# Attention with hashed masks and two gated layers: a head pair's queries prepared as a whole before its keys

## The chip, the cores and the metric

The kernel runs on one core of a Trainium2 chip. Its time is the device time of one execution in microseconds (us); a run is compared with runs of the other kernel on the same chip. The core has five engines with queues of their own, each in order: TensorE (PE, with its weight loads shown as PEld), VectorE (DVE), ScalarE (ACT), GpSimd (POOL) and SyncE (SP). SP issues all transfers (DMAs) of this kernel.

## The reference

```
q, k, v: 2 x 8 x 768 x 64; proj: 64 x 6
q_bits, k_bits = (q @ proj > 0), (k @ proj > 0)          # six hash bits a token
mask   = bucket(q_bits) == bucket(k_bits)                # all six bits agree
scores = q @ k.T / sqrt(64), -1e9 where not mask
attn   = exp(scores - max); attn /= (sum + 1e-9)
x      = attn @ v, heads side by side                    # 1536 x 512
h = x @ w_in (512 x 2048);   x = (h * cos(h)) @ w_out
g = x @ w_gate (512 x 1536); out = (silu(g) * (x @ w_val)) @ w_out2
```

## The kernel before

The 16 heads are worked in 8 pairs (NPAIR). A pair has 6 units, blocks of 128 queries; unit u belongs to pair u // 6, and each unit does both heads of its pair (j = 0, 1). `att_step(u)` issues one step of a software pipeline: scores of unit u, exponentials of u and u - 1, normalization of u - 1 (`row_norm`, on POOL), transposes of the probabilities of u - 2 (`p_transpose`, four groups of three on TensorE, one of the four copied out of PSUM by VectorE at L481, three by ScalarE), and the products with v for older units. The transposes share two PSUM buffers (`ps_t`), the scores two others (`ps_s`).

A float32 product is made exact enough by splitting an operand into a high part (rounded to float32r) and a low part (the remainder). The score product is two matrix products for each j: X with Y (L429; X holds the high and the low part of the queries, Y the high part of the keys twice) and Z with W (L431; Z holds the queries' high part and the query bits, W the keys' low part and the key bits). The bits are scaled so that a pair of tokens with different hash bits gets a huge negative score.

`prep(pr)` makes X, Y, Z and W of the next pair while the current one is worked. For queries and keys in turn it transposes the loaded rows on TensorE (L243), copies them to `raw` (tiles qT and kT) by ScalarE (L249) or VectorE (L253), and rounds them to `hi` (qH and kH, VectorE, L257). Then eight transfers spread the high parts (L260 to L263), in the order X, Z, Y, Y for one half of the tokens and again for the other. Then TensorE projects both (L285), VectorE compares with zero into the tile `bt` (L289), POOL scales it (L293), and eight small transfers put the bits into Z and W (L308). Last, POOL makes the low parts in place, qT - qH and kT - kH (L314), each with two transfers, to X and to W (L320).

The order on every engine is that of the program text: `prep` is a generator, and `fill` (called four times in a unit) takes one step of it and one step of the building of a dense weight. Before pair pr + 2 is prepared its queries and keys are loaded (`load_pair`, L222, emitted at the fifth unit of a pair). Every third unit from unit 8 on a weight is built, ten in all: ScalarE starts it (L125), VectorE finishes it in three operations (L140, L144, L148), and it is fetched three units earlier (L106, L110). SP therefore issues, in one line, the spreading of a pair, the loads of the one after it, and the weights.

Small per-row vectors (mn, the row maxima; sv, the sums; rv, the reciprocals) live in the pool `sm`.

Of the kernel before, what the change touches and what calls it, by code (L numbers as in the profile page):

```python
# [10 lines left out]
F32 = mybir.dt.float32  # L11
# [3 lines left out]
ALU = mybir.AluOpType  # L15
PSUM = bass.MemoryType.PSUM

P = 128
# [8 lines left out]
def lsh_attention_moe_moe2(  # L27
# [13 lines left out]
    nc = tc.nc  # L41
# [158 lines left out]
    ld = actx.enter_context(tc.tile_pool(name="ld", bufs=1))  # L200
    pre = actx.enter_context(tc.tile_pool(name="pre", bufs=1))
    pp = actx.enter_context(tc.tile_pool(name="pp", bufs=6))
    sm = actx.enter_context(tc.tile_pool(name="sm", bufs=8))

    pj0 = {nm: pre.tile([P, D], F32, tag="pj0" + nm, name="pj0" + nm) for nm in "qk"}
    pjs = pre.tile([P, NB], F32, tag="pjs", name="pjs")
# [20 lines left out]
    def prep_psum(pr, i, name):  # L227
        pool, tag = (ps_v, "av") if pr == 1 and i % 2 else (ps_p, "pp")
        return pool.tile([P, 512], F32, tag=tag, name=name)

    def prep(pr):
# [4 lines left out]
        X, Y, Z, W = (  # L236
            qk.tile([P, 2, S], F32R, tag=nm, bufs=2, name=f"{nm}{pr}") for nm in "XYZW"
        )
        for nm in ("q", "k"):
            for j in range(2):  # L240
                ps = prep_psum(pr, j, f"tr{nm}{pr}_{j}")
                for c in range(HB):
                    nc.tensor.transpose(  # L243
                        ps[:, c * P : (c + 1) * P],
                        nat[nm, pr][:, j, 2 * c : 2 * c + 2, :].rearrange("p c d -> p (c d)"),
                        ident,
                    )
                if nm == "q" or pr == 1:
                    nc.scalar.activation(  # L249
                        out=raw[nm][:, j, :], in_=ps[:, :HALF], func=AF.Copy, scale=TAKEN[nm]  # L250
                    )
                else:
                    nc.vector.tensor_copy(raw[nm][:, j, :], ps[:, :HALF])  # L253
                yield
                if pr > 1:
                    yield
            nc.vector.tensor_copy(hi[nm], raw[nm])  # L257
        for e in range(2):
            r, cs = slice(e * D, (e + 1) * D), slice(e * HALF, (e + 1) * HALF)
            nc.sync.dma_start(out=X[:D, :, cs].bitcast(F32), in_=hi["q"][r].bitcast(F32))  # L260
            nc.sync.dma_start(out=Z[:D, :, cs].bitcast(F32), in_=hi["q"][r].bitcast(F32))
            nc.sync.dma_start(out=Y[:D, :, cs].bitcast(F32), in_=hi["k"][r].bitcast(F32))
            nc.sync.dma_start(out=Y[D:, :, cs].bitcast(F32), in_=hi["k"][r].bitcast(F32))  # L263


        if pr == 1:
            bt = early.tile([P, 2, DM], F32, tag="raw", bufs=2, name="bt1")[:, :, :HALF]
            for j in range(2):
                ps = prep_psum(pr, j, f"pj1_{j}")
                for g, nm in enumerate(("q", "k")):  # L270
                    nc.tensor.matmul(
                        out=ps[g * D : (g + 1) * D, :HALF], lhsT=pj0[nm], rhs=raw[nm][:, j, :],
                        start=True, stop=True,
                    )
                nc.vector.tensor_scalar(
                    out=bt[:, j], in0=ps[:, :HALF], scalar1=0.0, scalar2=cvec[:, 1:2],
                    op0=ALU.is_gt, op1=ALU.subtract,
                )
# [17 lines left out]
        for g, dst in enumerate((Z, W)):  # L296
            rows = slice(D, D + 2 * NB)
            for e in range(2):
                cs = slice(e * HALF, (e + 1) * HALF)
                if pr == 1:  # L300
                    r0 = D * g + 32 * e
                    nc.sync.dma_start(
                        out=dst[rows, :, cs].bitcast(F32), in_=bt[r0 : r0 + 2 * NB]
                    )
                    continue
                for j in range(2):
                    r0 = 32 * (2 * g + j) + 2 * NB * e
                    nc.sync.dma_start(  # L308
                        out=dst[rows, j, cs].bitcast(F32), in_=bt[r0 : r0 + 2 * NB]
                    )  # L310
        yield
        yield
        for nm in ("q", "k"):
            nc.gpsimd.tensor_tensor(  # L314
                out=raw[nm], in0=raw[nm], in1=hi[nm].bitcast(F32), op=ALU.subtract
            )
            for e in range(2):
                cs = slice(e * HALF, (e + 1) * HALF)
# [4 lines left out]
        heads[pr] = (X, Y, Z, W)  # L323

    def prep_first():

# [20 lines left out]
                    )  # L347
            return ps

        def lows(eng, dst, j, nm, hi, e):  # L350
            r, cs = halves[e]
            eng.tensor_tensor(  # L352
                out=dst[:, j, cs], in0=raw[nm][r, j, :], in1=hi[:, j, cs].bitcast(F32),
                op=ALU.subtract,
            )

        ps = transposes(0)
        for j in range(2):
# [27 lines left out]
            lows(nc.gpsimd, W[:D], j, "k", Y[:D], 0)  # L386
            lows(nc.vector, X[D:], j, "q", X[:D], 0)
# [4 lines left out]
            for e in range(2):  # L392
# [8 lines left out]
            lows(nc.vector, W[:D], j, "k", Y[:D], 1)  # L401
            nc.vector.tensor_copy(Z[D : D + 2 * NB, j, :HALF], bt[: 2 * NB, j])
            yield
        for j in range(2):
            r, cs = halves[1]
            for dst in (X, Z):
                nc.scalar.activation(out=dst[:D, j, cs], in_=raw["q"][r, j, :], func=AF.Copy)
            nc.gpsimd.tensor_scalar(
                out=Z[D : D + 2 * NB, j, cs], in0=bt[32 : 32 + 2 * NB, j], scalar1=1.0,
                scalar2=1.0, op0=ALU.mult, op1=ALU.mult,  # L410
            )
            lows(nc.vector, X[D:], j, "q", X[:D], 1)
            yield

    scores = {}
# [469 lines left out]
```

## Time and profile before

| | us |
|---|---|
| median of 3 runs | 821.41 |
| lowest, highest | 819.27, 823.32 |
| the profiled execution | 822.72 |
| its span | 820.9 |
| TensorE busy in the span | 795.2 (97%) |
| VectorE, ScalarE, POOL busy | 466.5, 499.6, 454.1 |

In a row of the profile, L12 is line 12 of the kernel; an operation is named by what it writes and reads (out<-in). In a timeline a row begins with start and duration in us; a figure in square brackets is the idle time of the engine before it and what ended it. "issue" means that the engine waited for nothing that the profile shows by name. Transfers are shown by their issue on SP (SPq), not by their landing.

### The profile page before, as it was taken

How to read it: one execution, taken by the hardware profiler on the slowest of the kernel's cores; microseconds unless marked ns; L12 is line 12 of the kernel's file. 1: busy time of each engine (PE TensorE's matmuls, PEld its weight loads, DVE VectorE, ACT ScalarE, POOL GpSimd, SP SyncE). 2: the span in 40 equal slices, each digit the busy share in tenths (PEclk: the TensorE clock that was granted, in tenths of full speed). 3: DMA queues.
4: the chain of work that ended last, by engine and by line, in shares of the span. 5: the costliest groups of instructions: out<-in, count | busy, mean ns of one | idle time of the engine just before them, and what ended most of it. 6: DMA issues, size and time to landing. Idle time of an engine off the chain costs nothing.

```text
span 820.9 us, 11429 instructions
## 1 busy us (share of the span) xinstructions
PE 795.2 (97%) x3956; PEld 622.6 (76%) x3956; DVE 466.5 (57%) x865; ACT 499.6 (61%) x941; POOL 454.1 (55%) x394
## 2 busy tenths in 40 slices
PE   6899999998999999999999999999999999999998
PEld 4666666666675788888888888888888888888886
DVE  5888987887673999987755688752122111121112
ACT  5777767766685888887767777743334333343332
POOL 4754553653562677677776767744444444445440
PEclk8999999999999999999999999999999999999999
DMA  3745645644502455433220234300001000010001
GB/s 115 179 115 171 168 128 169 172 124 118 149 1 78 129 160 175 154 103 102 79 76 1 63 120 128 101 0 1 1 0 53 1 1 0 1 52 0 1 1 51
DMA packets 47049, 66.52 MB, mean 81 GB/s; under 512 B 3824, under 2 KB 41872, under 8 KB 46992
## 3 DMA queue, kind: packets, MB, share of 16 engines
q1 hardware_dynamic: 46992, 65.80, 27.4%
q8 instruction: 31, 0.51, 0.3%
q14 instruction: 26, 0.21, 0.1%
HBM read 45.09 MB, written 3.15 MB: 59 GB/s over the span
## 4 chain that ended last, share of the span: by engine, by line
PE 86%; DVE 6%; DMA 3%; issue 1%; POOL 1%; ACT 1%; SPq 1%; POOLq 0%; DVEq 0%; ACTq 0%
PE o L608 9%; PE o L610 9%; PE o L609 9%; PE av L491 6%; PE h L608 5%; PE h L610 5%; PE h L609 5%; PE t L473 5%; PE gate L609 4%; PE val L609 4%; PE val L608 4%; PE gate L608 4%; PE gate L610 4%; PE val L610 4%; PE s L429 3%; PE s L431 3%
## 5 line engine op out<-in xcount | busy, mean ns | idle before, releaser
L460 POOL TENSOR_SCALAR p<-p,rv 128x768 f32<-128x768 f32 x96 | 89.4, 942 | 106.3 <-DVE rv L457 99.2
L783 DVE TENSOR_TENSOR u<-val,sg 128x512 f32<-128x512 f32 x36 | 24.9, 692 | 198.7 <-ACT sg L777 188.4
L438 DVE TENSOR_SCALAR_CACHE_REDUCE p<-s 128x768 f32<-128x768 f32 x96 | 91.7, 955 | 46.7 <-PE s L431 38.4
L479 ACT ACTIVATE pt<-t 128x384 f32<-128x384 f32 x144 | 66.9, 486 | 53.6 <-PE t L473 53.5
L449 ACT ACTIVATE p<-p,mn 128x768 f32<-128x768 f32 x96 | 89.6, 934 | 9.4 <-DVE p L438 9.2
L473 PE MATMUL t<-ident,p 128*128 128x128 f32 x576 | 86.2, 274 | 6.0 <-DVE pt L481 5.6
L473 PEld LDWEIGHTS t<-ident,p 128*128 128x128 f32 x576 | 67.4, 140 | 17.1 <-DVE pt L481 7.5
L491 PE MATMUL av<-pt,vn 128*64 128x384 f32 x384 | 72.1, 498 | 0.0
L429 PE MATMUL s<-Y,X 128*128 128x512 f32 x192 | 59.2, 390 | 1.8 <-DVE X L352 1.8
L431 PE MATMUL s<-W,Z 76*128 76x512 f32 x192 | 51.2, 348 | 8.7 <-issue 3.8
L642 ACT ACTIVATE r<-r 128x512 f32<-128x512 f32 x48 | 30.4, 633 | 41.8 <-DVE r L634 41.8
L630 DVE SCALAR_TENSOR_TENSOR rf<-ki,h 128x512 f32<-128x512 int32 x46 | 32.0, 695 | 35.9 <-ACT ki L627 35.6
L429 PEld LDWEIGHTS s<-Y,X 128*128 128x128 f32 x192 | 29.3, 193 | 28.8 <-DVE pt L481 8.4
L125 ACT ACTIVATE w<-raw 128x512 f32<-128x512 f32 x68 | 44.6, 659 | 0.0
L491 PEld LDWEIGHTS av<-pt,vn 128*64 128x64 f32 x384 | 23.4, 136 | 25.8 <-issue 25.8
L654 DVE TENSOR_TENSOR g<-h,r 128x512 f32<-128x512 f32 x48 | 33.1, 689 | 16.9 <-ACT r L643 16.6
L431 PEld LDWEIGHTS s<-W,Z 76*128 76x128 f32 x192 | 30.3, 194 | 15.1 <-issue 7.9
L144 DVE SCALAR_TENSOR_TENSOR bw<-w,bw 128x512 int32<-128x512 int32 x55 | 38.0, 691 | 1.2
L140 DVE TENSOR_SCALAR bw<-raw 128x512 int32<-128x512 int32 x55 | 38.0, 691 | 1.0
L148 DVE SCALAR_TENSOR_TENSOR w<-raw,bw 128x512 int32<-128x512 int32 x55 | 37.5, 683 | 0.9
L643 ACT ACTIVATE r<-r,halfpi 128x512 f32<-128x512 f32 x48 | 34.8, 724 | 1.6
L627 ACT ACTIVATE ki<-h 128x512 int32<-128x512 f32 x48 | 28.3, 590 | 11.2 <-PE h L610 11.2
(1872 smaller groups left out, 2298.7 us busy)
## 6 DMA issues: line engine op xcount, KB each, us to landing
raw<-in_moe_w_out_dram SPq DMA_DIRECT2D x28, 512.0 KB
raw<-in_moe_w_in_dram SPq DMA_DIRECT2D x16, 512.0 KB
raw<-in_moe_w_gate_dram SPq DMA_DIRECT2D x12, 512.0 KB
raw<-in_moe_w_val_dram SPq DMA_DIRECT2D x12, 512.0 KB
Y<-kH SPq DMA_DIRECT2D x28, 192.0 KB
vn<-in_v_dram SPq DMA_DIRECT2D x8, 384.0 KB
out_dram<-ot SPq DMA_DIRECT2D x12, 256.0 KB
qn<-in_q_dram SPq DMA_DIRECT2D x7, 384.0 KB
```

Of the source, the lines that this page charges most:

```text
L125: nc.scalar.activation(out=t, in_=raws[i][:, :, 1].bitcast(F32), func=AF.Copy, scale=2.0**-112)
L429: nc.tensor.matmul(out=ps[:, ks], lhsT=X[:, j, qs], rhs=Y[:, j, ks], start=True, stop=False)
L431: nc.tensor.matmul(out=ps[:, ks], lhsT=Z[:KZ, j, qs], rhs=W[:KZ, j, ks], start=False, stop=True)
L438: nc.vector.tensor_scalar(out=pt, in0=ps[:, :S], scalar1=-MASKED, scalar2=None, op0=ALU.min, op1=ALU.min, accum_out=mn,)
L449: nc.scalar.activation(out=pt, in_=pt, func=AF.Exp, bias=nbias.pop((u, j)), scale=-1.0, accum_out=sums[u][:, j : j + 1],)
L460: nc.gpsimd.tensor_scalar(out=pt, in0=pt, scalar1=rv[:, j : j + 1], scalar2=1.0, op0=ALU.mult, op1=ALU.mult)
L473: nc.tensor.transpose(ps[:, c * P : (c + 1) * P], src[:, kb * P : (kb + 1) * P], ident)
L479: nc.scalar.activation(out=o, in_=s3, func=AF.Copy)
L491: nc.tensor.matmul(out=ps[j * D : (j + 1) * D, :HALF], lhsT=nat["v", pr][:, j, BLOCKS[kb], :], rhs=pts[half, j][:, kb, :], start=(kb == 0) ...
L608: nc.tensor.matmul(out=out_ap, lhsT=sh, rhs=mh, start=first, stop=False)
L609: nc.tensor.matmul(out=out_ap, lhsT=sh, rhs=ml, start=False, stop=False)
L610: nc.tensor.matmul(out=out_ap, lhsT=sl, rhs=mh, start=False, stop=last)
```

## The change

For pairs 2 to 7 `prep` now does all of the queries first: after the rounding of the queries come four transfers (X, X, Z, Z), the low part on POOL and its two transfers, and only then the keys: transposes, copies, rounding, and four transfers to Y. The bits and the keys' low part follow, the latter two steps of the generator earlier against the normalizations. The queries' low part is no longer made in place; it gets a tile of its own (qL, tag `low`, one buffer), and `bt` is now the first half of a tile of the same tag. Pair 1 keeps its order except that of the eight transfers. The pool `sm` has four buffers instead of eight. The two functions `bits` and `lows` hold what stood in the body of `prep`.

```
-    sm = actx.enter_context(tc.tile_pool(name="sm", bufs=8))
+    sm = actx.enter_context(tc.tile_pool(name="sm", bufs=4))
...
             nc.vector.tensor_copy(hi[nm], raw[nm])
-        for e in range(2):
-            r, cs = slice(e * D, (e + 1) * D), slice(e * HALF, (e + 1) * HALF)
-            nc.sync.dma_start(out=X[:D, :, cs].bitcast(F32), in_=hi["q"][r].bitcast(F32))
-            nc.sync.dma_start(out=Z[:D, :, cs].bitcast(F32), in_=hi["q"][r].bitcast(F32))
-            nc.sync.dma_start(out=Y[:D, :, cs].bitcast(F32), in_=hi["k"][r].bitcast(F32))
-            nc.sync.dma_start(out=Y[D:, :, cs].bitcast(F32), in_=hi["k"][r].bitcast(F32))
+            for dst in (X[:D], Z[:D]) if nm == "q" else (Y[:D], Y[D:]):
+                for e in range(2):
+                    r, cs = slice(e * D, (e + 1) * D), slice(e * HALF, (e + 1) * HALF)
+                    nc.sync.dma_start(
+                        out=dst[:, :, cs].bitcast(F32), in_=hi[nm][r].bitcast(F32)
+                    )
+            if pr > 1 and nm == "q":
+                lows(pr, nm, raw, hi)
...
-            bt = pre.tile([P, HALF], F32, tag="bt", name=f"bt{pr}")
+            bt = pre.tile([P, 2, HALF], F32, tag="low", name=f"bt{pr}")[:, 0]
...
+        bits(pr, bt)
         yield
         yield
-        for nm in ("q", "k"):
-            nc.gpsimd.tensor_tensor(
-                out=raw[nm], in0=raw[nm], in1=hi[nm].bitcast(F32), op=ALU.subtract
-            )
-            for e in range(2):
-                cs = slice(e * HALF, (e + 1) * HALF)
-                dst = X[D:, :, cs] if nm == "q" else W[:D, :, cs]
-                nc.sync.dma_start(out=dst.bitcast(F32), in_=raw[nm][e * D : (e + 1) * D])
+        for nm in ("q", "k") if pr == 1 else ("k",):
+            lows(pr, nm, raw, hi)
             yield
             yield
...
+    def lows(pr, nm, raw, hi):
+
+        X, _, _, W = heads[pr]
+        t = raw[nm]
+        if pr > 1 and nm == "q":
+            t = pre.tile([P, 2, HALF], F32, tag="low", name=f"{nm}L{pr}")
+        nc.gpsimd.tensor_tensor(out=t, in0=raw[nm], in1=hi[nm].bitcast(F32), op=ALU.subtract)
+        for e in range(2):
+            cs = slice(e * HALF, (e + 1) * HALF)
+            dst = X[D:, :, cs] if nm == "q" else W[:D, :, cs]
+            nc.sync.dma_start(out=dst.bitcast(F32), in_=t[e * D : (e + 1) * D])
```

On TensorE, VectorE and ScalarE the same instructions stand in the same order; only their waits change. The order differs on POOL and SP, alike for pairs 2 to 7. Shown is the preparation of pair 2.

POOL, from the normalizations of unit 6 on (p are probabilities, rv their reciprocals), before:

```order
L460 TENSOR_SCALAR p_0_536<-p_0_536,rv_605 128x768
L460 TENSOR_SCALAR p_1_578<-p_1_578,rv_605 128x768
L460 TENSOR_SCALAR p_0_602<-p_0_602,rv_669 128x768
L460 TENSOR_SCALAR p_1_639<-p_1_639,rv_669 128x768
L293 TENSOR_SCALAR bt_683<-bt_683,svec 128x384
L314 TENSOR_TENSOR qT_544<-qT_544,qH_545 128x768
L460 TENSOR_SCALAR p_0_666<-p_0_666,rv_752 128x768
L460 TENSOR_SCALAR p_1_725<-p_1_725,rv_752 128x768
L314 TENSOR_TENSOR kT_546<-kT_546,kH_547 128x768
```

and after, the same place:

```order
L473 TENSOR_SCALAR p_0_536<-p_0_536,rv_605 128x768
L473 TENSOR_SCALAR p_1_578<-p_1_578,rv_605 128x768
L332 TENSOR_TENSOR qL_615<-qT_544,qH_545 128x768
L473 TENSOR_SCALAR p_0_602<-p_0_602,rv_677 128x768
L473 TENSOR_SCALAR p_1_647<-p_1_647,rv_677 128x768
L315 TENSOR_SCALAR bt_687<-bt_687,svec 128x384
L332 TENSOR_TENSOR kT_546<-kT_546,kH_547 128x768
L473 TENSOR_SCALAR p_0_674<-p_0_674,rv_756 128x768
L473 TENSOR_SCALAR p_1_729<-p_1_729,rv_756 128x768
```

The queries' subtraction moved up by one unit, and the keys' subtraction moved ahead of the two normalizations that stood before it.

SP, from the weight fetch ahead of the spreading of pair 2 to the loads for pair 3, before:

```order
L110 DMA raw_652<-in_moe_w_in_dram 128x4x256
L260 DMA X_548<-qH_545 64x2x384
L261 DMA Z_550<-qH_545 64x2x384
L262 DMA Y_549<-kH_547 64x2x384
L263 DMA Y_549<-kH_547 64x2x384
L260 DMA X_548<-qH_545 64x2x384
L261 DMA Z_550<-qH_545 64x2x384
L262 DMA Y_549<-kH_547 64x2x384
L263 DMA Y_549<-kH_547 64x2x384
L308 DMA Z_550<-bt_683 12x384 x4
L308 DMA W_551<-bt_683 12x384 x4
L320 DMA X_548<-qT_544 64x2x384 x2
```

and after:

```order
L281 DMA X_548<-qH_545 64x2x384 x2
L281 DMA Z_550<-qH_545 64x2x384 x2
L336 DMA X_548<-qL_615 64x2x384 x2
L110 DMA raw_660<-in_moe_w_in_dram 128x4x256
L281 DMA Y_549<-kH_547 64x2x384 x4
L246 DMA Z_550<-bt_687 12x384 x4
L246 DMA W_551<-bt_687 12x384 x4
L336 DMA W_551<-kT_546 64x2x384 x2
L222 DMA qn_790<-in_q_dram 128x2x384
```

All six transfers of the queries now stand ahead of the keys' and the bits'; the keys' low part (which before followed the last row shown) stands right behind the bits; the second weight fetch went behind the queries.

VectorE at the comparison into bt, with the semaphores that an instruction waits for in square brackets (DMAHW is one of the eight semaphores that the transfers take in turn), before:

```order
L457 RECIPROCAL rv_669<-rv_669 128x2 [waits DVE_49]
L257 CAST kH_547<-kT_546 128x768 [waits DMAHW5_49,DMAHW4_49]
L289 TENSOR_SCALAR bt_683<-pj_684,cvec 128x384 [waits PE_49]
L481 COPY pt_0_660<-t_0_1_701 128x3x128 [waits PE_49]
L140 TENSOR_SCALAR raw_472<-raw_472 128x512 [waits DMAHW4_49,Activation_49]
L438 TENSOR_SCALAR p_1_725,mn_1_726<-s_1_712 128x768 [waits PE_49,Pool_49]
```

and after:

```order
L470 RECIPROCAL rv_677<-rv_677 128x2 [waits DVE_49]
L277 CAST kH_547<-kT_546 128x768 [waits DMAHW7_49,DMAHW6_49]
L311 TENSOR_SCALAR bt_687<-pj_688,cvec 128x384 [waits DMAHW1_49,DMAHW2_49,PE_49,Pool_49]
L494 COPY pt_0_668<-t_0_1_705 128x3x128 [waits PE_49]
L140 TENSOR_SCALAR raw_472<-raw_472 128x512 [waits DMAHW4_49,Activation_49]
L451 TENSOR_SCALAR p_1_729,mn_1_730<-s_1_716 128x768 [waits PE_49]
```

The order is the same, but the comparison has gained the waits for DMAHW1 and DMAHW2, which are here the semaphores of the two transfers X<-qL, and for POOL.

## Rows read from the trace of the kernel before

**Rows 1.** The page, part 4: the chain that ended last, by engine.

```profile
PE 86%; DVE 6%; DMA 3%; issue 1%; POOL 1%; ACT 1%; SPq 1%; POOLq 0%; DVEq 0%; ACTq 0%
```

**Rows 2.** Busy time by stretch: stretch, length, engines (instructions), granted clock, DMA share, GB/s.

```profile
300.00:500.00 200.00, 200.00 (x884) 165.62 (x884) 151.46 (x234) 154.43 (x270) 142.39 (x112) 1.00 0.32 101
```

**Rows 3.** TensorE's groups, 40 to 245 us: busy us, mean ns | idle before, releasers.

```profile
L431 PE MATMUL s<-W,Z 76*128 76x512 f32 (+1 forms) x165 | 43.2, 342 | 6.2 <-issue 3.8 <-DMA qn<-in_q_dram 2.4
...
L243 PE MATMUL trq<-ident,qn 128*128 128x128 f32 x36 | 6.1, 277 | 1.3 <-DMA qn<-in_q_dram 1.3
```

**Rows 4.** Timeline of TensorE at the boundaries before pair 2 and near 190 us.

```profile
67.30 0.62 PE L429 MATMUL s<-Y,X 128*128 128x512 f32 x2
67.75 0.52 PE L431 MATMUL s<-W,Z 76*128 76x512 f32 x2
...
68.68 0.60 PE L429 MATMUL s<-Y,X 128*128 128x512 f32 x2
69.46 0.59 PE L431 MATMUL s<-W,Z 76*128 76x512 f32 x2 [0.18 <-issue]
...
193.16 0.58 PE L431 MATMUL s<-W,Z 76*128 76x512 f32 x2 [2.38 <-DMA qn<-in_q_dram]
```

**Rows 5.** Timeline of SP, the spreading of pair 2: start and time of issue.

```profile
47.65 0.60 SPq L260 DMA_DIRECT2D X<-qH  x1
48.34 1.00 SPq L261 DMA_DIRECT2D Z<-qH  x1
...
57.20 3.24 SPq L308 DMA_DIRECT2D Z<-bt  x4
...
63.58 1.37 SPq L320 DMA_DIRECT2D X<-qT  x2
65.05 1.25 SPq L320 DMA_DIRECT2D W<-kT  x2
```

**Rows 6.** Timeline of POOL in the preparation of pair 2, and pair 7's bit scaling.

```profile
47.20 2.03 POOL L460 TENSOR_SCALAR p<-p,rv 128x768 f32<-128x768 f32 x2 [3.24 <-DVE rv L457]
...
54.15 0.75 POOL L293 TENSOR_SCALAR bt<-bt,svec 128x384 f32<-128x384 f32 x1
54.87 1.83 POOL L314 TENSOR_TENSOR qT<-qT,qH 128x768 f32<-128x768 f32 x1
...
207.26 0.58 POOL L293 TENSOR_SCALAR bt<-bt,svec 128x384 f32<-128x384 f32 x1
```

**Rows 7.** Busy time by stretch, while two and six large transfers run (columns as above).

```profile
49.00:51.00 2.00, 2.00 (x20) 1.73 (x22) 1.73 (x5) 1.50 (x3) 0.24 (x1) 1.00 0.83 184
...
53.50:59.50 6.00, 5.79 (x37) 4.05 (x35) 5.65 (x11) 2.78 (x6) 3.39 (x4) 1.00 0.89 200
```

**Rows 8.** Timeline of VectorE from the comparison of pair 2 on.

```profile
52.43 0.61 DVE L289 TENSOR_SCALAR bt<-pj,cvec 128x384 f32<-128x384 f32 x1
52.96 0.55 DVE L481 COPY pt<-t 128x384 f32<-128x384 f32 x1
53.42 1.03 DVE L140 TENSOR_SCALAR raw<-raw 128x512 int32<-128x512 int32 x1
54.73 0.96 DVE L438 TENSOR_SCALAR_CACHE_REDUCE p<-s 128x768 f32<-128x768 f32 x1 [0.28 <-PE s L431]
...
55.61 1.63 DVE L144 SCALAR_TENSOR_TENSOR w<-w,raw 128x512 int32<-128x512 int32 x1
...
59.05 0.54 DVE L481 COPY pt<-t 128x384 f32<-128x384 f32 x1
```

**Rows 9.** Timeline of TensorE's probability transposes: pair 2, then pair 7.

```profile
54.44 0.82 PE L473 MATMUL t<-ident,p 128*128 128x128 f32 x6
...
59.64 0.55 PE L473 MATMUL t<-ident,p 128*128 128x128 f32 x3 [0.35 <-DVE pt L481]
...
207.54 0.82 PE L473 MATMUL t<-ident,p 128*128 128x128 f32 x6
```

**Rows 10.** Timeline of VectorE at the comparison of pair 7.

```profile
205.54 0.62 DVE L289 TENSOR_SCALAR bt<-pj,cvec 128x384 f32<-128x384 f32 x1
```

More of the change, by code (lines that the diff above doesn't have):

```diff
@@ L229, in prep_psum, with bits @@
         return pool.tile([P, 512], F32, tag=tag, name=name)
+    def bits(pr, bt):
+        _, _, Z, W = heads[pr]
+        rows = slice(D, D + 2 * NB)
+        for g, dst in enumerate((Z, W)):
+            for e in range(2):
+                cs = slice(e * HALF, (e + 1) * HALF)
+                if pr == 1:
+                    r0 = D * g + 32 * e
+                    nc.sync.dma_start(
+                        out=dst[rows, :, cs].bitcast(F32), in_=bt[r0 : r0 + 2 * NB]
+                    )
+                    continue
+                for j in range(2):
+                    r0 = 32 * (2 * g + j) + 2 * NB * e
+                    nc.sync.dma_start(
+                        out=dst[rows, j, cs].bitcast(F32), in_=bt[r0 : r0 + 2 * NB]
+                    )
     def prep(pr):
@@ L235, in prep @@
             hi[nm] = pre.tile([P, 2, HALF], F32R, tag=nm + "H", name=f"{nm}H{pr}")
-        X, Y, Z, W = (
+        X, Y, Z, W = heads[pr] = [
             qk.tile([P, 2, S], F32R, tag=nm, bufs=2, name=f"{nm}{pr}") for nm in "XYZW"
-        )
+        ]
         for nm in ("q", "k"):
@@ L257, in prep @@
             nc.vector.tensor_copy(hi[nm], raw[nm])
-        for e in range(2):
-            r, cs = slice(e * D, (e + 1) * D), slice(e * HALF, (e + 1) * HALF)
-            nc.sync.dma_start(out=X[:D, :, cs].bitcast(F32), in_=hi["q"][r].bitcast(F32))
-            nc.sync.dma_start(out=Z[:D, :, cs].bitcast(F32), in_=hi["q"][r].bitcast(F32))
-            nc.sync.dma_start(out=Y[:D, :, cs].bitcast(F32), in_=hi["k"][r].bitcast(F32))
-            nc.sync.dma_start(out=Y[D:, :, cs].bitcast(F32), in_=hi["k"][r].bitcast(F32))
+            for dst in (X[:D], Z[:D]) if nm == "q" else (Y[:D], Y[D:]):
+                for e in range(2):
+                    r, cs = slice(e * D, (e + 1) * D), slice(e * HALF, (e + 1) * HALF)
+                    nc.sync.dma_start(
+                        out=dst[:, :, cs].bitcast(F32), in_=hi[nm][r].bitcast(F32)
+                    )
+            if pr > 1 and nm == "q":
+                lows(pr, nm, raw, hi)
         if pr == 1:
@@ L295, in prep @@
         )
-        for g, dst in enumerate((Z, W)):
-            rows = slice(D, D + 2 * NB)
-            for e in range(2):
-                cs = slice(e * HALF, (e + 1) * HALF)
[L300 to L310, printed above, removed]
+        bits(pr, bt)
         yield
         yield
-        for nm in ("q", "k"):
-            nc.gpsimd.tensor_tensor(
-                out=raw[nm], in0=raw[nm], in1=hi[nm].bitcast(F32), op=ALU.subtract
-            )
-            for e in range(2):
-                cs = slice(e * HALF, (e + 1) * HALF)
-                dst = X[D:, :, cs] if nm == "q" else W[:D, :, cs]
-                nc.sync.dma_start(out=dst.bitcast(F32), in_=raw[nm][e * D : (e + 1) * D])
+        for nm in ("q", "k") if pr == 1 else ("k",):
+            lows(pr, nm, raw, hi)
             yield
             yield
-        heads[pr] = (X, Y, Z, W)
+    def lows(pr, nm, raw, hi):
[4 more added lines that the diff above has]
+        nc.gpsimd.tensor_tensor(out=t, in0=raw[nm], in1=hi[nm].bitcast(F32), op=ALU.subtract)
+        for e in range(2):
+            cs = slice(e * HALF, (e + 1) * HALF)
+            dst = X[D:, :, cs] if nm == "q" else W[:D, :, cs]
+            nc.sync.dma_start(out=dst.bitcast(F32), in_=t[e * D : (e + 1) * D])
     def prep_first():
@@ L348, in transposes, with rest_of @@
             return ps
-        def lows(eng, dst, j, nm, hi, e):
+        def rest_of(eng, dst, j, nm, hi, e):
             r, cs = halves[e]
@@ L385, in prep_first @@
             yield
-            lows(nc.gpsimd, W[:D], j, "k", Y[:D], 0)
-            lows(nc.vector, X[D:], j, "q", X[:D], 0)
+            rest_of(nc.gpsimd, W[:D], j, "k", Y[:D], 0)
+            rest_of(nc.vector, X[D:], j, "q", X[:D], 0)
             nc.vector.tensor_scalar(
@@ L400, in prep_first @@
                     nc.scalar.activation(out=dst, in_=src, func=AF.Copy, scale=-BIG)
-            lows(nc.vector, W[:D], j, "k", Y[:D], 1)
+            rest_of(nc.vector, W[:D], j, "k", Y[:D], 1)
             nc.vector.tensor_copy(Z[D : D + 2 * NB, j, :HALF], bt[: 2 * NB, j])
@@ L411, in prep_first @@
             )
-            lows(nc.vector, X[D:], j, "q", X[:D], 1)
+            rest_of(nc.vector, X[D:], j, "q", X[:D], 1)
             yield
```

## The prediction

> **What bounds the kernel now.** The chain of work that ended last was read first: 86% of it is TensorE, so a change pays or costs only where TensorE waits [rows 1]. The table by stretch comes second. Between 300 and 500 us TensorE is busy for all 200 us at a granted clock of 1.00, so the two dense layers can neither absorb a delay of the attention nor use up a gain: whatever the attention gains or loses arrives at the end in full [rows 2]. The attention ends near 260 us, and there the waits are small. Third come TensorE's groups between 40 and 245 us. Only two have idle time worth naming: 6.2 us before the second score product (L431, operands W and Z) and 1.3 us before the transposes of the next queries (L243) [rows 3].
>
> The timeline shows what these are. Ordinarily the W-Z product starts 0.45 us after the X-Y product (67.30, 67.75). At the first unit of pair 2 it starts 0.78 us after it (68.68, 69.46) [rows 4]. There the last prepared operands, W from the low part of the keys, were issued only at 65.05 us, behind eight small bit transfers (57.20 on) and the queries' low part (63.58) [rows 5]. The queries of the next pair are loaded behind those again. So the pair boundary is a wait for a late SP queue, six times.
>
> **The change part by part.**
>
> *Relief at the boundary.* The lost time is 0.78 - 0.45 = 0.33 us where the row counts 0.18 us idle: the idle figure misses 0.15 us, because the product before ends late. The 6.2 us are six boundaries and the 1.3 us three, so the loss is 7.5 + 9 x 0.15 = 8.9 us. After the change the queries' low part leaves before the bits, and the keys' low part stands on POOL right behind the bits, ahead of two normalizations. SP then issues in pair 2: bits from about 56.9, eight of them in 6.4 us (57.20 to 63.58), keys' low part at about 63.3 [rows 5]. That is 1.8 us earlier, while TensorE reaches the boundary later (below, 2.3 us). Four microseconds of lead cover every boundary, so I take all 8.9 us. Bounds: 7.5 (the idle figures alone) to 8.9.
>
> *The price: VectorE waits for a transfer.* The queries' low part goes no longer in place but into a tile "low", of which there is one buffer, and the bit tile bt shares it. So the comparison that writes bt (L289, now L311) has to wait until both transfers X<-qL have read that buffer and landed; in the order of the changed kernel it has gained exactly those two waits. VectorE works in order: behind it stand the copy of a transposed block (L481), three weight operations (L140, L144, L148) and the row maxima (L438). TensorE waits for these through its two transpose buffers.
>
> When do they land? The first X<-qH goes out at 47.65 [rows 5]. With all queries together, four transfers follow each other, and the low part joins as fifth and sixth: POOL finishes the normalizations at 47.20 + 2.03 = 49.23 and needs 1.83 us for the subtraction, 51.06 [rows 6]. The six are then limited by the transfer rate: two such transfers (192 KB each) took the 2.0 us from 49.0 to 51.0, and the 6 us with six of them ran at 200 GB/s, a share of 0.89, which is 0.98 us each [rows 7]. Four in a row, issued from 63.58 on, had landed when the product started at 69.46: 5.85 us [rows 4, 5]. Two more make 7.8 us. So the sixth lands at 47.65 + 7.8 = 55.45; with 0.15 us for the waits in a row bt starts at 55.6 instead of 52.43, a delay D of 3.2 us [rows 8].
>
> The Trainium skill ("DMA: Bandwidth & Descriptors", section Bandwidth) states that transfers from SBUF to SBUF are bound by the fabric's 435 GB/s. By it each would take an estimated 0.45 us, the six would be limited by their issue, and the sum would be that of the rival "shorter wait" below; the 200 GB/s of [rows 7] speak against it.
>
> What does D cost TensorE? I replay VectorE from the start B of the comparison [rows 8]. The copy follows at B + 0.53 and is done at B + 1.08. TensorE's fourth transpose group of that unit needs its buffer: it stood at 54.44 + 0.33 = 54.77 [rows 9] and now comes at 55.63 + 1.14 = 56.8, 2.0 us late. Then the weight operations. L140 starts at B + 0.99. Before, it took 1.03 us beside POOL's normalizations and ended 0.3 us after them; now POOL's bit scaling (0.58 us where nothing is beside it [rows 6]) ends at B + 1.23, so L140 ends at B + 1.55. POOL's subtraction for the keys, 1.83 us, then runs to B + 3.4. The row maximum goes from B + 1.55, L144 from B + 2.43. Before, L144 took 1.63 us and ended 0.54 us after POOL's subtraction (54.87 + 1.83); the same lag gives B + 3.95. From its end to the second copy before there are 59.05 - 57.24 = 1.81 us, so this copy starts at B + 5.75. Before it stood at B + 6.62 and already held TensorE up (59.64, idle 0.35) [rows 8, 9]. TensorE thus loses D - 0.87 = 2.3 us a pair. Five pairs (2 to 6) carry weight operations there: 11.5 us. Pair 7 carries none: its comparison at 205.54 moves to 208.74, the copy ends at 209.8, and TensorE's group from 207.54 + 0.33 = 207.87 comes at 209.9, 2.0 us late; nothing further is late [rows 9, 10]. Sum 13.5 us. Bounds: none at all (a wait that is met in time) to five times 3.6 and 2.0, 20 us (the second rival).
>
> *What costs nothing.* Four buffers instead of eight for mn, sv and rv: a vector comes round again after two units (mn) or four (sv, rv), a unit being some 4.9 us (54.77 to 59.64 [rows 9]), and its reader is done within one. POOL's subtraction for the queries, moved up a unit, falls into an idle time of POOL like the 3.24 us before 47.20 [rows 6]. If that cover fell, VectorE could lose up to those 1.83 us, ahead of a comparison that waits anyway. Pair 1 keeps its POOL order; only SP's order within a burst changes, for operands first read at the next boundary. The second weight load of a pair now waits in SP behind the queries; the program fetches it three units ahead of its use, some 15 us.
>
> *Sum.* 13.5 - 8.9 = +4.6 us. On the profiled execution, 822.72 us, that is 827.3; the median of the three runs is 821.41, on which it is 826.0. About 0.5%, 4.1 us, is what a measurement of this kernel can tell from no change, so the forecast is slower, but near that bound.
>
> **The rivals.**
>
> *Shorter wait, no change.* If the low part's transfers overlap the four before instead of queuing behind them, the last one needs only its own time. It is issued at about 51.8, and the lone second transfer needed 51.0 - 48.34 = 2.7 us [rows 5, 7], with completion and waits about 54.9: D is 2.5, a pair loses 1.6 us and the last 1.3, together 9.3, and 821.41 + 0.4 gives 821.8. It decides the sign where D is below about 2.4 us. For it: nothing else is on the queues then. Against it: the full share at 200 GB/s.
>
> *L140 loses to POOL.* If POOL's key subtraction starts before L140, that one waits for the subtraction's end: L140 ends 0.3 us after it at B + 3.7, L144 starts at B + 4.6 and no longer waits (0.6 us), and the second copy stands at B + 7.0. A pair loses 3.6 us, the sum is 20 - 8.9 = +11, 832.5 us. Against it: in [rows 6, 8] L140 ended before the bit scaling went on, which took 0.75 instead of 0.58 us.
>
> *Relief without a price, faster.* If the wait were met in time, 821.41 - 8.9 gives 812.5. It needs the sixth transfer to land by 52.4, 4.8 us after the first is issued; four needed 5.85.
>
> *The change doesn't do what it says.* If the boundary stays late for another reason (a transfer that lags, as at 193.16, with 2.38 us idle the worst of the six [rows 4]), half of the relief is lost: +9, 830.4.
>
> **How the numbers follow.** Forecast as summed (824 to 828.5): 0.48. Shorter wait (820 to 824): 0.22. L140 loses (830 to 834): 0.17. Half the relief: 0.07. No price: 0.06. Slower by over 0.5% means above 825.5: 0.31 of the forecast's 0.48 and the two dear rivals, 0.55. Within 0.5%: 0.39. Faster: 0.06. The range is 819.5 to 832.5: it leaves out the free case and the far ends of the dear ones.
>
> **What the changed profile would show.** VectorE's comparison L311 idle for about 3 us, six times, released by X<-qL; 2.0 us of TensorE idle before transposes at the copy right behind it, and up to 0.8 more, by the second copy, in five pairs; no idle time left before the W-Z product and the queries' transposes; DMA busy without a gap for 6 us from the first X<-qH. The forecast is wrong if the comparison waits less than 2.4 us, if L144 still takes 1.6 us and the second copy is later than B + 6.3, or if the W-Z product still waits at the boundaries.

## The result

The changed kernel takes **827.85 us** (median; 826.41 to 828.53), the kernel before 820.43 us beside it (819.27 to 823.32). The ratio is 1.0084, interval 1.0061 to 1.0108. It is slower by 0.8%, as forecast in sign, and 1.9 us above the forecast of 826.0. The two profiled executions, 828.53 us (span 826.7) and 822.72 us, differ by 5.8 us, the medians by 7.4 us: the profiled execution before lies 2.3 us above the median of its kernel. What is traced below is the 5.8 us.

### The profile page after: what moved, and what is told of

Read it like the earlier page. It is cut to its first block, busy times and chain, and to the rows that moved or that the text cites. A ratio compares the mean times of both kernels' runs of the same rounds, so it can differ in the third digit from the quotient of the medians.

```text
span 826.7 us, 11419 instructions
## 1 busy us (share of the span) xinstructions
PE 799.4 (97%) x3956; PEld 623.2 (75%) x3956; DVE 459.1 (56%) x865; ACT 500.3 (61%) x941; POOL 455.4 (55%) x394
## 4 chain that ended last, share of the span: by engine, by line
PE 89%; DVE 5%; ACT 2%; DMA 1%; issue 1%; POOL 1%; SPq 0%; POOLq 0%; DVEq 0%
PE o L623 9%; PE o L621 9%; PE o L622 9%; PE av L504 7%; PE t L486 7%; PE h L621 5%; PE h L622 5%; PE h L623 5%; PE val L623 4%; PE gate L623 4%; PE s L442 4%; PE val L622 4%; PE gate L622 4%; PE val L621 4%; PE gate L621 4%; PE s L444 3%
## 5 line engine op out<-in xcount | busy, mean ns | idle before, releaser
L486 PE MATMUL t<-ident,p 128*128 128x128 f32 x576 | 89.6, 278 | 16.1 <-DVE pt L494 12.0
L144 DVE SCALAR_TENSOR_TENSOR bw<-w,bw 128x512 int32<-128x512 int32 x55 | 38.0, 691 | 1.2
L140 DVE TENSOR_SCALAR bw<-raw 128x512 int32<-128x512 int32 x55 | 38.0, 691 | 1.0
```

The source lines that it names most:

```text
L486: nc.tensor.transpose(ps[:, c * P : (c + 1) * P], src[:, kb * P : (kb + 1) * P], ident)
```

## The profile after

The chain of waits, by engine, answers to [rows 1]:

```profile
PE 89%; DVE 5%; ACT 2%; DMA 1%; issue 1%; POOL 1%; SPq 0%; POOLq 0%; DVEq 0%
```

TensorE's groups between 40 and 262 us (columns as in [rows 3]), first of the kernel before, which [rows 3] do not hold, then of the changed one:

```profile
L473 PE MATMUL t<-ident,p 128*128 128x128 f32 x528 | 78.9, 274 | 2.1 <-DVE pt L481 1.7 <-ACT pt L479 0.4
```

```profile
L486 PE MATMUL t<-ident,p 128*128 128x128 f32 x519 | 80.9, 278 | 12.0 <-DVE pt L494 7.8 <-ACT pt L492 3.8
...
L444 PE MATMUL s<-W,Z 76*128 76x512 f32 (+1 forms) x166 | 43.1, 341 | 0.0
...
L263 PE MATMUL trq<-ident,qn 128*128 128x128 f32 x33 | 5.4, 272 | 0.0
```

The 6.2 and 1.3 us of [rows 3], at the W-Z product and the queries' transposes, are gone. In their place the probability transposes wait 12.0 us instead of 2.1. So one wait was exchanged for another, as the prediction said. VectorE's waits in the same stretch name the cause (columns: waited for, us in total, times, longest):

```profile
DVE bt L311 <- PE t L486: 11.0, 3, 3.7
DVE bt L311 <- DMA X<-qL: 8.7, 3, 2.9
```

Both rows are one wait, the comparison that writes bt, six times. In three of them the view names a transpose of TensorE that happens to end just then. The comparison reads nothing of it: what it reads of TensorE are the projections pj, which ended 3.7 to 4.5 us before it in all six pairs. What ended last there too was the transfer X<-qL. Pair 2 shows it, SP first, then VectorE, its keys' cast in the kernel before, and TensorE (compare [rows 5, 8, 9]):

```profile
46.36 2.17 SPq L281 DMA_DIRECT2D X<-qH  x2
48.62 1.25 SPq L281 DMA_DIRECT2D Z<-qH  x2
49.96 1.25 SPq L336 DMA_DIRECT2D X<-qL  x2
...
56.23 3.17 SPq L246 DMA_DIRECT2D Z<-bt  x4
...
62.54 1.37 SPq L336 DMA_DIRECT2D W<-kT  x2
```

```profile
50.67 0.56 DVE L277 CAST kH<-kT 128x768 fp32r<-128x768 f32 x1
54.90 0.62 DVE L311 TENSOR_SCALAR bt<-pj,cvec 128x384 f32<-128x384 f32 x1 [3.68 <-PE t L486]
...
55.90 0.59 DVE L140 TENSOR_SCALAR raw<-raw 128x512 int32<-128x512 int32 x1
...
57.27 1.43 DVE L144 SCALAR_TENSOR_TENSOR w<-w,raw 128x512 int32<-128x512 int32 x1
...
60.50 0.54 DVE L494 COPY pt<-t 128x384 f32<-128x384 f32 x1
```

```profile
51.96 0.56 DVE L257 CAST kH<-kT 128x768 fp32r<-128x768 f32 x1
```

```profile
49.99 0.49 PE L307 MATMUL pj<-kT,pjk 128*32 128x384 f32 x2
...
54.22 0.55 PE L486 MATMUL t<-ident,p 128*128 128x128 f32 x3 [0.58 <-ACT pt L492]
...
61.09 0.55 PE L486 MATMUL t<-ident,p 128*128 128x128 f32 x3 [1.58 <-DVE pt L494]
...
70.13 0.59 PE L442 MATMUL s<-Y,X 128*128 128x512 f32 x2
70.56 0.52 PE L444 MATMUL s<-W,Z 76*128 76x512 f32 x2
```

The second transfer X<-qL is recorded as landed at 54.77 us, and the comparison starts at 54.90, 4.23 us after the start of the keys' cast; before, it started 0.47 us after it (51.96, 52.43). The delay D is thus 3.76 us. At the boundary W-Z follows X-Y by 0.43 us, without a wait.

**Where the 5.8 us are.** The starts of the X-Y products of the attention's units were compared, one trace minus the other. The difference moves at four kinds of place, and stays at 5.85 us from pair 7's boundary to the attention's end:

| place | us |
|---|---|
| the first 22 us | -1.25 |
| preparation of pairs 2 to 7 (TensorE's loss S) | 2.73, 2.91, 2.74, 2.12, 2.01, 0.96: +13.47 |
| boundaries of pairs 2 to 7 | -1.17, -1.04, -1.66, -1.70, -2.61, -1.37: -9.55 |
| behind the losses of pairs 3 and 4 | +1.56, +1.62: +3.2 |

The last line is TensorE's granted clock (busy time by stretch, columns as in [rows 2]):

```profile
85.00:90.00 5.00, 4.22 (x26) 2.33 (x25) 3.20 (x6) 1.64 (x3) 2.49 (x2) 1.00 1.07 232
90.00:95.00 5.00, 3.35 (x16) 2.59 (x17) 3.78 (x10) 3.45 (x9) 1.84 (x3) 0.84 0.24 47
95.00:100.00 5.00, 5.00 (x28) 3.31 (x27) 3.10 (x8) 2.79 (x7) 1.79 (x2) 0.82 0.82 241
...
125.00:130.00 5.00, 3.73 (x19) 2.51 (x21) 3.71 (x12) 4.11 (x9) 2.71 (x4) 0.75 0.28 60
130.00:135.00 5.00, 5.00 (x32) 3.25 (x30) 2.74 (x8) 2.97 (x7) 0.87 (x1) 0.91 0.97 303
```

Twice it is at its lower level, 1.2 GHz, for a while, behind a wait of 1.58 us at the second copy. Elsewhere in the attention, past its start, it is 1.00. In the first of these stretches a group of six transposes takes 1.48 instead of 0.82 us.

## The experiments

The theory: the wait for X<-qL is the whole price, and TensorE loses in each pair what the comparison is late, less about 1 us. The rivals: the moved work itself costs (transfers in a row, POOL beside VectorE), or the relief only exists because TensorE is late.

### e1_bits_in_qT, the wait taken away: bits in the used-up queries' tile

```
-            bt = pre.tile([P, 2, HALF], F32, tag="low", name=f"bt{pr}")[:, 0]
+            bt = raw["q"][:, 0]
```

> The changed kernel, with the bit tile bt placed in the queries' tile qT, which is used up by then, instead of in the buffer "low". The comparison then waits for no transfer; everything else of the change stays. Theory (the wait for X<-qL is the whole price): the comparison starts 0.5 us after the keys' cast again instead of 3.4 to 4.3 us, the 13.5 us that TensorE lost in the preparations of pairs 2 to 7 go, and so do the two stretches of 3.4 us at the half granted clock (3.2 us), which stood right behind such stalls; the boundaries keep their 9.6 us of relief and the start its 1.25 us. From the 822.7 us of the profiled execution before that is 822.7 - 9.6 - 1.25 = 811.9, in the median 809.6 to 811, about 1.2% faster than before. Rival A (the price is the moved work itself, six transfers in a row and POOL's subtraction beside VectorE, and the buffer only its visible place): the copies stay late and the time stays at 824 to 828. Rival B (the relief only came because TensorE was late at the boundary): the stalls go, but the W-Z product waits again, 818 to 821.

Measured: 813.61 us (812.81 to 814.61), ratio to before 0.9907 (0.9891 to 0.9924). The comparison starts 0.47 us after the keys' cast in all six pairs, TensorE loses 0.68 us in the six preparations together, the boundaries keep 9.2 us of relief, and the clock is 1.00 from 20 us on. Both rivals fall: the same moved work without the wait is a gain. VectorE in pair 2, and TensorE's groups, 40 to 262 us:

```profile
50.64 0.56 DVE L277 CAST kH<-kT 128x768 fp32r<-128x768 f32 x1
51.12 0.61 DVE L311 TENSOR_SCALAR qT<-pj,cvec 128x384 f32<-128x384 f32 x1
```

```profile
L486 PE MATMUL t<-ident,p 128*128 128x128 f32 x525 | 78.4, 274 | 2.7 <-DVE pt L494 2.4 <-ACT pt L492 0.3
...
L444 PE MATMUL s<-W,Z 76*128 76x512 f32 (+1 forms) x166 | 42.8, 339 | 0.0
```

### e2_low_before_Z, a shorter wait: the low part ahead of Z

```
-            for dst in (X[:D], Z[:D]) if nm == "q" else (Y[:D], Y[D:]):
+            for i, dst in enumerate((X[:D], Z[:D]) if nm == "q" else (Y[:D], Y[D:])):
+                if pr > 1 and nm == "q" and i == 1:
+                    lows(pr, nm, raw, hi)
...
-            if pr > 1 and nm == "q":
-                lows(pr, nm, raw, hi)
```

> The changed kernel with one row moved: the two transfers of the queries' low part (X<-qL) are issued ahead of the two Z<-qH instead of behind them. Theory (TensorE loses what the comparison is late, less 1.02 us): the low part leaves SP when POOL has made it, as before, but two transfers stand ahead of it in the queue instead of four. Two transfers of 0.98 us fewer: the comparison's delay falls from 2.9 to 3.8 us by 1.2 to 2.0 us, TensorE loses six times that less, 7 to 12 us, and with shorter stalls the two stretches at the half clock (3.2 us) may go: 814 to 821 us. Rival A (the place in the queue does not matter, because all six land together or because POOL's subtraction is what is late): 826 to 828. Rival B (Z now comes late): the X-Y products start as in the changed kernel, but the W-Z product waits at the boundary.

Measured: 823.60 us (822.60 to 825.91), ratio 1.0024 (1.0013 to 1.0036). That misses the 814 to 821 of the theory, because its D was wrong: it fell only to 2.65 to 2.87 us in pairs 2 to 6, and rose to 4.47 in pair 7. SP now stands until POOL has made the low part (X<-qL at 50.58 in pair 2), and from there the transfer's own time counts: 2.88 and 3.18 us from issue to landing, with only the two X<-qH ahead of it, the first of which had landed. In pair 7 the second X<-qL lands 4.96 us after its issue, its first piece 2.81 us after it; why that one lags is open. The rule of the theory held: TensorE lost D less 0.86 to 1.00 us in pairs 2 to 6. The half clock is gone as well. The W-Z product waits at no boundary, but here that goes with TensorE's lateness: the last W<-kT leaves SP 13.3 to 14.2 us after the keys' cast, hardly earlier than before the change (13.7 to 14.2).

### e3_low_twice, a longer wait: the low part sent twice

```
-            nc.sync.dma_start(out=dst.bitcast(F32), in_=t[e * D : (e + 1) * D])
+            for _ in range(2 if pr > 1 and nm == "q" else 1):
+                nc.sync.dma_start(out=dst.bitcast(F32), in_=t[e * D : (e + 1) * D])
```

> The changed kernel with both transfers X<-qL issued twice in pairs 2 to 7 (the same bytes to the same place). The buffer "low" is read until the fourth has landed, so the comparison's delay grows by about two transfers of 0.98 us, 2.0 us. Theory (TensorE loses the comparison's delay, less 1.02 us): six times 2.0 us more, 12 us, so about 840 us; more if the half-clock stretches grow in number (each cost 1.6 us). Rival (TensorE has other work for a delay beyond 3.5 us, or loses at the copies only by the buffer it happens to have): less than half of that, under 834 us.

Measured: 864.05 us (862.23 to 865.05), ratio 1.0516 (1.0494 to 1.0538), 36 us more than the changed kernel, where 12 were expected. A repeat writes where the one before wrote. The program orders two writes of one place by a wait, so SP held the repeat until the first had landed (in pair 2 at 54.06 us, the repeat left at 54.08): the four issues took 7.63 us, and D became 8.6 to 9.7 us instead of some 5.4. VectorE's wait, TensorE in pair 2, and the stretches around it:

```profile
DVE bt L311 <- DMA X<-qL: 52.4, 6, 9.6
```

```profile
61.92 0.90 PE L487 MATMUL t<-ident,p 128*128 128x128 f32 x3 [4.94 <-DVE pt L495]
```

```profile
55.00:60.00 5.00, 1.74 (x10) 1.20 (x10) 0.00 (x0) 0.68 (x2) 0.00 (x0) 0.78 0.47 115
60.00:65.00 5.00, 3.08 (x11) 1.27 (x11) 4.19 (x7) 1.40 (x3) 2.53 (x2) 0.50 1.02 243
65.00:70.00 5.00, 5.00 (x25) 3.86 (x25) 3.67 (x9) 3.16 (x7) 1.79 (x2) 0.69 0.30 62
```

TensorE loses 8.4 to 9.6 us a pair, D less 0.02 to 0.23. The rule alone gives about 0.9 less than D in pairs 2 to 6; the difference goes with the lower clock level, which sets in during all six waits here and outlasts them, in pair 2 for 10.3 us by the three rows (shares of 0.44, 1.0 and 0.62 of 5 us). The rival (a long wait is partly free) falls.

### e4_small_bufs, four small buffers alone

```
-    sm = actx.enter_context(tc.tile_pool(name="sm", bufs=8))
+    sm = actx.enter_context(tc.tile_pool(name="sm", bufs=4))
```

> The kernel before with one number changed: the pool of the small row vectors has four buffers instead of eight. It tells apart where the 1.25 us come from that the changed kernel is ahead by after its first 22 us. If four buffers cost nothing and gain nothing, as forecast: 820.4 us, within 0.3%, and the start as before. If the smaller pool is what moved the start: 819.2 us and the half-clock stretch of the start ends 3 us earlier. If a vector comes round too early, ScalarE or VectorE shows waits of mn, sv or rv and it is slower than 822.

Measured: 822.61 us (819.30 to 826.53), ratio 1.0005 (0.9987 to 1.0023): it costs nothing that can be measured. It also bears on the 1.25 us of the start: here, with the order of the kernel before, the start is 0.37 us ahead of the profiled execution before, and in the other kernels of this study 0.2 to 1.3 us, whatever their order in pair 1. The changed kernel itself was 1.25 us ahead in one profiled execution and 0.53 us in the other (e7_after_again). So it is mostly a difference between executions; its cause is open, and nothing ties it to the change.

### e5_queries_first, one part alone: queries first

The low parts stay in place and behind the bits; bt has its own buffer (against the changed kernel):

```
-            if pr > 1 and nm == "q":
-                lows(pr, nm, raw, hi)
...
-            bt = pre.tile([P, 2, HALF], F32, tag="low", name=f"bt{pr}")[:, 0]
+            bt = pre.tile([P, HALF], F32, tag="bt", name=f"bt{pr}")
...
-        for nm in ("q", "k") if pr == 1 else ("k",):
+        for nm in ("q", "k"):
...
-        if pr > 1 and nm == "q":
-            t = pre.tile([P, 2, HALF], F32, tag="low", name=f"{nm}L{pr}")
```

> The kernel before with one part of the change alone: the four transfers of the queries' cast are issued ahead of the keys' four. Both low parts stay in place and behind the bits, bt has its own buffer, no wait is added (the four small buffers are in as well; they measured 1.0005). It tells which part brings the relief at the boundaries. Theory (SP is late because it stands waiting for the keys' cast with three of the queries' transfers still unissued): SP sends these in that idle time, the bits start about 1.6 us earlier (at 55.6 instead of 57.2 us in pair 2) and so does everything behind them; most of the 9.5 us at the boundaries go, and the time is 813.5 to 816. Rival (the relief comes from the low part of the queries leaving early and the keys' low part standing earlier on POOL): the W-Z product keeps its waits and the time is 821 to 823.

Measured: **812.89 us** (812.52 to 813.23), ratio 0.9891 (0.9871 to 0.9911): faster than both kernels, and the whole relief, 9.56 us at the six boundaries. SP in pair 2, and W-Z between 40 and 262 us:

```profile
47.20 1.79 SPq L281 DMA_DIRECT2D X<-qH  x2
49.08 1.25 SPq L281 DMA_DIRECT2D Z<-qH  x2
...
52.10 2.57 SPq L281 DMA_DIRECT2D Y<-kH  x4
54.77 3.17 SPq L246 DMA_DIRECT2D Z<-bt  x4
...
62.55 1.25 SPq L332 DMA_DIRECT2D W<-kT  x2
```

```profile
L440 PE MATMUL s<-W,Z 76*128 76x512 f32 (+1 forms) x168 | 43.3, 339 | 0.0
```

Before, SP sent one X and one Z (47.65, 48.34 in [rows 5]), stood until the keys' cast, and had two more of the queries' transfers behind it. Here all four leave in that idle time, and what follows the keys' cast is earlier: bits at 54.77 instead of 57.20, the last W<-kT landed at 66.86 instead of 69.37 us. This execution was 0.45 us ahead at that point; the other 2.0 us are the change's. Counted from the keys' cast, SP issues the last W<-kT after 13.7 to 14.2 us in the kernel before, after 11.7 to 12.3 us here, and after 10.8 to 12.7 us with the low part early as well (bits in qT): the early low part adds no steady lead to that of the queries (later in four pairs, earlier in two).

### e6_low_early and e8_low_early_free, the other part alone: low parts early, casts in the old order

```
-            for dst in (X[:D], Z[:D]) if nm == "q" else (Y[:D], Y[D:]):
-                for e in range(2):
...
-            if pr > 1 and nm == "q":
-                lows(pr, nm, raw, hi)
+        for e in range(2):
+            r, cs = slice(e * D, (e + 1) * D), slice(e * HALF, (e + 1) * HALF)
+            for dst, nm in ((X[:D], "q"), (Z[:D], "q"), (Y[:D], "k"), (Y[D:], "k")):
...
+        if pr > 1:
+            lows(pr, "q", raw, hi)
...
-            bt = pre.tile([P, 2, HALF], F32, tag="low", name=f"bt{pr}")[:, 0]
+            bt = raw["q"][:, 0]
```

> The other part alone: the eight transfers of the casts in the order of the kernel before (queries and keys mixed, from the keys' cast on), but the low part of the queries in the buffer "low" and ahead of the bits, the keys' low part right behind the bits, and the bits in qT, so that no wait for a transfer is added. Theory (the relief is SP's, by issuing in its idle time): SP has the same 18 transfers to issue between the keys' cast and the boundary, and W<-kT leaves at about 65 us as before; only the two X<-qL no longer stand right ahead of it. Relief 0 to 3 us: 819.5 to 823. Rival (the relief comes from the low parts): 813 to 815.

Measured: 826.99 us (826.68 to 827.26), ratio 1.0064 (1.0045 to 1.0082); neither theory had that. The edit brought a wait of its own: the bits go into qT, so the comparison has to wait for POOL's subtraction, and that now stands behind two normalizations.

```profile
DVE qT L311 <- POOL qL L332: 20.8, 6, 3.5
```

As a test of the price this is the best one: the same comparison is late by 3.56 us in every pair, with no transfer in it, and TensorE loses 2.56 to 2.60 us in pairs 2 to 6 and 1.44 in pair 7. The price is the lateness of the comparison, whatever holds it. As a test of the relief it was spoilt: the W-Z product no longer waited, but TensorE came 2.6 us later to each boundary, so nothing was left to wait for (in pair 2 the last W<-kT landed at 68.73 us, W-Z started at 71.25). In e8_low_early_free the accidental wait was taken out (against e6_low_early):

```
+            if pr > 1 and nm == "q":
+                low = pre.tile([P, 2, HALF], F32, tag="low", name=f"qL{pr}")
+                nc.gpsimd.tensor_tensor(
+                    out=low, in0=raw[nm], in1=hi[nm].bitcast(F32), op=ALU.subtract
+                )
...
-            lows(pr, "q", raw, hi)
+            for e in range(2):
+                cs = slice(e * HALF, (e + 1) * HALF)
+                nc.sync.dma_start(out=X[D:, :, cs].bitcast(F32), in_=low[e * D : (e + 1) * D])
```

> e6_low_early without the wait that it had by accident: there the comparison, which writes into qT, waited 3.5 us for POOL's subtraction of the queries, which POOL had only after two normalizations. Here POOL has the subtraction where the changed kernel has it, right behind the queries' cast, and only the two transfers X<-qL stay where e6 has them, behind the eight transfers of the casts. No wait is added, so what is left is the relief by the low parts alone. Theory (the relief is SP's, by issuing in its idle time): SP's row is as in e6, where W<-kT landed 0.64 us earlier than in the kernel before (68.73 to 69.37), 0.2 us of that by its earlier start; the W-Z product still waits at the boundaries, the relief is 0.2 to 0.6 us a boundary, 1 to 4 us, and TensorE's waits at the copies are gone: 818.5 to 821.5. Rival (the low parts bring the relief too, once TensorE is not late by itself): 812 to 814, no idle time before W-Z.

Measured: 821.18 us (819.60 to 823.40), ratio 0.9998 (0.9983 to 1.0012). The low parts bring no relief that can be measured; the interval leaves room for 1.4 us at most. The boundary waits are there again (40 to 262 us), 6.1 us in sum instead of 7.5 and shared out otherwise: the W-Z product waits less than before, the queries' transposes more, for loads that stand behind W<-kT in SP's line. SP sends the keys' low part at 65.05 us, as in [rows 5]:

```profile
L451 PE MATMUL s<-W,Z 76*128 76x512 f32 (+1 forms) x168 | 43.7, 341 | 2.3 <-DMA W<-kT 1.9 <-issue 0.2
L263 PE MATMUL trq<-ident,qn 128*128 128x128 f32 x36 | 6.2, 280 | 3.8 <-DMA qn<-in_q_dram 3.8
```

```profile
56.91 1.74 SPq L292 DMA_DIRECT2D X<-qL  x2
58.74 3.17 SPq L246 DMA_DIRECT2D Z<-qT  x4
61.95 2.99 SPq L246 DMA_DIRECT2D W<-qT  x4
65.05 1.37 SPq L343 DMA_DIRECT2D W<-kT  x2
```

### e7_after_again, the changed kernel once more

Nothing is edited; this is a second profiled execution.

> The changed kernel unchanged, beside these two on the same chip, for a second profile of it. Theory (TensorE's losses of 13.5 us come from the wait and are the same in every execution; the half-clock stretches behind them are not): the comparison is late by 2.9 to 3.8 us again in six pairs and TensorE loses 2.0 to 2.9 us again in five of them and about 1.0 us in the last, but the stretches at half clock may stand behind other pairs or be missing; each that is there costs 1.6 us, and the time is 824 to 829. Rival (the stretches belong to the kernel): they stand behind pairs 3 and 4 again.

Measured: 828.29 us (827.20 to 829.14), ratio 1.0078 (1.0059 to 1.0098). D and the losses repeat within 0.1 us, but for pair 2, where both are 0.5 us smaller (table below; 13.0 us in sum). The rival on the clock is right: the two stretches stand behind pairs 3 and 4 again and cost 1.57 and 1.61 us.

```profile
90.00:95.00 5.00, 3.35 (x17) 2.51 (x16) 3.97 (x9) 3.45 (x8) 2.07 (x3) 0.86 0.25 49
95.00:100.00 5.00, 5.00 (x28) 3.39 (x27) 3.00 (x7) 2.85 (x8) 1.79 (x2) 0.80 0.70 198
125.00:130.00 5.00, 3.44 (x17) 2.58 (x19) 4.05 (x12) 4.10 (x9) 2.42 (x3) 0.77 0.22 50
130.00:135.00 5.00, 5.00 (x30) 3.16 (x28) 2.48 (x6) 2.69 (x7) 1.16 (x2) 0.89 0.95 286
```

### All delays together

D is how much later than 0.47 us behind the keys' cast the comparison starts, S what the unit starts lose in that preparation, without the stretches at half clock except in the last row:

| kernel | D, pairs 2 to 6 | S, pairs 2 to 6 | D, S in pair 7 |
|---|---|---|---|
| bits in qT | 0.0 | 0.27, 0.10, 0.10, 0.10, 0.11 | 0.0, 0.0 |
| low before Z | 2.65, 2.66, 2.76, 2.87, 2.80 | 1.65, 1.78, 1.88, 2.01, 1.90 | 4.47, 2.45 |
| changed | 3.76, 3.80, 3.65, 3.02, 2.91 | 2.73, 2.91, 2.74, 2.12, 2.01 | 3.04, 0.96 |
| changed, again | 3.24, 3.79, 3.65, 3.02, 2.94 | 2.22, 2.89, 2.77, 2.14, 2.02 | 3.04, 0.96 |
| low early (POOL) | 3.56 in each | 2.56, 2.56, 2.58, 2.56, 2.60 | 3.56, 1.44 |
| low twice | 8.62, 8.65, 8.81, 8.56, 8.64 | 8.39, 8.54, 8.61, 8.47, 8.54 | 9.66, 9.64 |

In the rows with a delay of 2.6 to 3.8 us, S is D less 0.86 to 1.03 in pairs 2 to 6, and D less 2.02 to 2.12 in pair 7.

## Why the prediction was right, and where it was not

- **What bounds the kernel** held. The 5.85 us of the attention's units are the 5.8 us between the two profiled executions; the dense layers took nothing.
- **The relief** was sized well, 8.9 us against 9.55, 0.65 us above the upper bound. The term too small is the 0.15 us that each of the nine waits was to cost beyond its idle figure (7.48 us in sum). It was 0.23 us: at the boundary of pair 2 the W-Z product starts 0.17 us later than its figure says, and the transposes behind it follow after 0.42 instead of 0.36 us (kernel before against queries first). And the step that explains the relief left out the part that is enough by itself. It counted the low part ahead of the bits and the keys' low part behind them; these two with the casts in the old order give 0.9998. The queries' four casts leaving before the keys' cast, which it did not count, give the whole relief alone (0.9891). Whether the low part's two transfers, sent in that idle time without them, would do it too is not shown.
- **That VectorE waits for a transfer** held: six waits of the comparison, released by X<-qL, and 813.61 us without them.
- **D** was forecast at 3.2 us for all. It measured 2.9 to 3.0 in pairs 5 to 7 and 3.65 to 3.80 in pairs 2 to 4; the mis-sized term is the landing of the sixth transfer, forecast 7.8 us after the first issue and measured at 8.1 to 8.4 in pairs 2 to 4 (in pair 2 46.36 to 54.77) and at 7.6 to 7.7 in pairs 5 to 7. In pair 2 X<-qH took 2.17 us to issue and the low part left only at 49.96. In pair 3 the four Z and low transfers took 3.8 to 4.3 us from issue to landing, in pairs 5 to 7 3.3 to 3.9.
- **TensorE loses D less 0.87** held in size for pairs 2 to 6 (0.86 to 1.03). The replay of VectorE behind it held too: L140 took 0.59 us and was not held up by POOL, L144 took 1.43, and the second copy came 5.60 us after the comparison (forecast 5.75).
- **The place** of that loss was wrong. The prediction put 2.0 us at the transposes right behind the first copy. There TensorE waited 0.58 us, and for ScalarE's copy; the large wait, 1.58 us, is at the second copy. In the changed program the two transpose buffers are dealt out in another order: the group that waited for the semaphore of VectorE's copy before (at 54.77) now waits for that of ScalarE's (at 54.22). The wait of 0.58 us for ScalarE stands in every profiled execution with a late comparison and in none without. The prediction had assumed that the group would wait for VectorE's copy. In pairs 2 to 6 this should change nothing, since by the replay the second copy sets the sum either way; no run tests it. In pair 7, where no weight operations hold up the second copy, it does: 0.96 us instead of 2.0.
- **The sum** of 13.5 us measured 13.47, but by luck, through two misses of opposite sign: 12.51 against 11.5 in pairs 2 to 6, 0.96 against 2.0 in pair 7.
- **The clock** was missing from the sum: 3.2 us behind pairs 3 and 4. With 0.65 us more relief and the 1.25 us of the start, it is what separates +4.6 from the +5.85 of the two profiled executions.
- **What costs nothing** held: the four small buffers measured 1.0005, and with the rest of the change in place but the wait gone TensorE lost 0.68 us in the six preparations (bits in qT).
- **The rivals.** "Shorter wait" rested on transfers that overlap, and it priced the last at 2.7 us to its landing by the end of a stretch of [rows 7]; in that trace it landed at 51.47, 3.13 us after its issue. From 46.40 to 54.80 us the queues moved 182 GB/s, near the 200 of [rows 7]. Even with the low part moved ahead, D stayed at 2.65 us or more. "L140 loses to POOL" did not come. "Relief without a price" is what the kernels without the wait are, 812.89 and 813.61 us, near the 812.5 it was priced at; it needed another place for the bits, or the low parts left where they were.

## What to carry to other kernels

When a change moves several things at once and its diff adds one wait, price the wait and the moves separately, and build the version that has the moves without the wait: here the order of four transfers was the whole gain (0.9891), and the buffer that two tiles share the whole loss. The in-order queue gained here from what could be issued while it would have stood waiting; look there before moving work on other engines. And a wait that goes away because its engine comes later is no relief: ask when the operand lands, not only whether somebody still waits for it.

## What the runs showed of the hardware

- TensorE's clock fell to 1.2 GHz behind some waits and not behind others that look alike. In the first profile of the changed kernel it stayed at 1.00 behind waits of 0.58 and 1.58 us in pair 2 and fell behind the same two in pair 4; the second profile has the fall at pairs 3 and 4 again. With 0.58, 0.46 and 1.45 to 1.48 us (low early, pairs 2 to 6) it never fell; with waits of 4.9 to 6.1 us (low twice, six pairs) it always did. What decides between them is open; where it fell behind the shorter waits of the changed kernel it cost 1.6 us each time.
- The boundary wait of the kernel before also differs between executions. With four small buffers, the profiled execution lost 2.6 us more at one boundary (waits of 1.00 and 0.56 us, and a granted clock of 0.73 in the 5 us behind). That goes with the spread, 819.43 to 825.75 us for the kernel before beside it and 812.52 to 813.23 with queries first. It is not all of it: low before Z waits at no boundary and spreads from 822.60 to 825.91.
- A transfer of 192 KB between two places in SBUF took 2.81 to 2.93 us from the start of its issue to its landing where none of its kind was under way when it was issued (low twice, twelve transfers). By the Trainium skill ("DMA: Bandwidth & Descriptors", section Anatomy of one DMA — SWDGE (gpsimd) path) a DMA costs some 2.0 us and its bytes at 436 GB/s, an estimated 2.45 us for these. The page measured another path of issue; the trace is 0.4 to 0.5 us above it, and decides.
